# Load order at the start, first units between stages, and the place of the sums in a fused Hyena filter and maxout FFN kernel

## The chip, the cores and the metric

The kernel runs on one core of a Trainium2 chip. The metric is the device time in microseconds (us) of one execution. Every operand is fp32.

## What is computed

The reference, cut to what matters (B = 4, S = 12544, D = 128, filter order 64, d_ff 768):

```python
h_mlp = np.maximum(pos_emb @ w1, 0.0) @ w2
window = np.exp(-0.01 * pos)[:, None]
h_filt = h_mlp * window
u = x * v
L = 2 * S
Uf = np.fft.rfft(u, n=L, axis=1)
Hf = np.fft.rfft(h_filt, n=L, axis=0)
y = np.fft.irfft(Uf * Hf[None, :, :], n=L, axis=1)[:, :S, :]
attn = x * y
...
h = np.maximum(np.maximum(attn @ w1, attn @ w2), attn @ w3)   # moe_w1, moe_w2, moe_w3
return h @ w_out
```

So each batch gets a long convolution along the sequence with a filter that an MLP makes from positions, a gate by x, and then a feed-forward layer that takes the elementwise maximum of three products.

## The kernel before, in words

The Fourier transforms are written as matmuls on TensorE (PE): a first transform over one index of the sequence, a twiddled second one for each of 45 pairs of frequencies, the product with the filter's spectrum, a third one, and an inverse. Instructions are issued by hand in program order (`manual_schedule`), so each engine works through its own queue in the order in which the code emits. A load or store belongs to the queue of the engine that issues it: SyncE (SP), ScalarE (ACT) or GpSimd (POOL). VectorE (DVE) issues none. A tile is one buffer of a pool; a new tile waits until the old user of its buffer is done.

**Start (lines 256 to 343, 859 to 905).** Positions (`pos`, in the storage of `specH`) come in eight pieces, four on SP's and four on ACT's queue (L293); `w1` comes ahead of them on ACT's (L289). On POOL's queue come the window, `eye`, `back`, then the tables `f1h` and `f1q` and two copies of `w2` (L283 to L299). PE meanwhile runs warm-up matmuls on zeros (L156 with `pw`), turns the window (`window_back`) and runs three more warm-ups. Then come eight groups `mlp_in(i)` (L332, pos times w1, into two PSUM tiles `pm`), each followed by `mlp_out(i)` on DVE (L340: relu and window, two instructions). After the last one, sixteen "quads" (`first_halves`, L165) transform the filter, and in between the first units of u = x * v of batch 0 are multiplied on DVE (`u_mul`, L365), turned on PE (`turn2`, eight transposes at L370, one ACT copy at L852) and later transformed by quads as well. A unit is a group of 4 channels-by-position blocks; there are 32 units in a batch.

**Filter stage (lines 996 to 1031).** For each of 45 pairs: `s_second`, `s_filter`, `s_store` make and store the filter's spectrum (`hd`), and `g_second`, `g_third` and their DVE and ACT work convolve batch 0 (stored to `zd`). Near its end the first six units of batch 1 (`EARLY = 6`) are loaded and multiplied and four of them turned.

**Drain (lines 1030 to 1042).** After the last pair the code runs `unit(0)` to `unit(5)` (the first transform of those units: `u_first`, L417, ACT copy L426, DVE add and subtract L428), turns units 4 and 5, and folds two weight matrices into `lin` (`fold`, six transposes and six products). Then the pools of this part are closed and the main loop's are opened.

**Main loop (lines 1068 to 1101).** For three batches, 32 tiles each, six slots f in a tile. A tile is loaded (`t_load`: `zt`, `xT`), two tiles ahead; `t_sums` makes its sum and difference (L678 and L679, or L682 with a sign), `t_last` inverts it on PE and gates it with xT on DVE (L700). In slot f, `up` runs eight `hps` matmuls (L156), a relu on ACT (L710) and a maximum on DVE (L713) over three rotating PSUM banks, and `down` four `ops` matmuls for the slot two back. Beside them `conv_steps` has planned the next batch's convolution: a list of steps by slot (192 in a batch), of which units come first, and pairs from slot `s0`. The planner keeps a `load` per slot and puts `q_re`, `q_im` and `q_unfold` (DVE work of a pair) where it is least. The sums of the next tile are emitted at f = 0, ahead of `up`, on POOL as long as units are worked on (`i * NF <= s0`) and on DVE after that; on the last tile of a batch at f = 3. `t_last` follows at f = 3, 4 or 2.

**Last stage (from L1102).** The last batch's FFN, in another form; the change does not touch it.

Of the kernel before, what the change touches and what calls it, by code (L numbers as in the profile page):

```python
# [91 lines left out]
def kernel(  # L92
# [163 lines left out]
    inp0 = fin.enter_context(tc.tile_pool(name="inp0", bufs=3))  # L256
    sml = fin.enter_context(tc.tile_pool(name="sml", bufs=1))
    mps = ExitStack()
    fps = mps.enter_context(tc.tile_pool(name="fps0", bufs=4, space=PSUM))

# [25 lines left out]
    nc.gpsimd.dma_start(eye[:], eye_d)  # L286
    nc.gpsimd.dma_start(back[:].rearrange("p r t -> p (r t)"), back_d)
    for h in range(2):
        nc.scalar.dma_start(w1_sb[64 * h:64 * h + 64], w1[:, :])  # L289
    cuts = (0, 11, 21, 31, HH)  # L290
    for j, (lo_, hi_) in enumerate(zip(cuts, cuts[1:])):
        for h in range(2):
            (nc.scalar if (h + j) % 2 else nc.sync).dma_start(  # L293
                pos[64 * h:64 * h + 64, lo_ * P:hi_ * P],
                posT[:, (h * HH + lo_) * P:(h * HH + hi_) * P])
    nc.gpsimd.dma_start(f1h[:], f1h_d)
    nc.gpsimd.dma_start(w2_in[0:FO], w2[:, :])
    nc.gpsimd.dma_start(w2_in[FO:P], w2[:, :])
    nc.gpsimd.dma_start(f1q[:], f1_d)  # L299
    for r in range(2):  # L300
        nc.scalar.copy(winT[:, r, 0:64], warm[:, 0:64])

    def warm_up(n):

        ps = fps.tile([P, 1024], FP32, tag="cv", name="pw", bufs=2)
        for _ in range(n):
            halves_mm(ps[:, 0:256], warm[:, 0:P], warm[:], True, True)

    def window_back():
        pw = fps.tile([P, 1024], FP32, tag="cv", name="pw", bufs=2)  # L310
# [270 lines left out]
    def conv_steps(b, done):  # L581


        out = []

        def at(slot, late, fn, *args):
            out.append((slot, late, len(out), fn, args))

        per_pair = 170 / (NK + LATE + 0.6 * (NU - done))
        for u in range(done, NU):
            s = (u - done) * 0.6 * per_pair + 9
            at(max(0, int(s) - 9), 0, u_load, b, u)
            at(int(s) - 6, 0, u_mul, u)
            at(int(s) - 5, 0, u_planes, u)
            at(int(s) - 4, 0, u_dma, u)
            at(int(s), 0, u_join, u)
            at(int(s + 1), 1, u_first, u)
        s0 = int((NU - done - 1) * 0.6 * per_pair + 9) + 6  # L600

        def start(x):
            return s0 + int(x // 2 * 2 * per_pair)

        load = [(1.2 if i % NF == 3 else 0.6) + (1.4 if i % NF == 0 and i > s0 else 0)
                for i in range(NT * NF)]
        for x in range(NK + LATE):
            s = start(x)
            load[s] -= 1.2
            load[s + 1 + x % 2] += 1.4  # L610

        def emptiest(among, cost):
            s = min(among, key=lambda i: load[i])
            load[s] += cost
            return s

        for x in range(NK + LATE):
            s, odd = start(x), x % 2
# [24 lines left out]
        return slots, {start(x) + 1 for x in range(NK + LATE)}, s0  # L643


    N = 4 * NB
# [24 lines left out]
                              x[:, 4 * i:4 * i + 8, c, b, :])  # L671
        xTs[b, i], xTs[b, i + 1] = xT[:, 0], xT[:, 1]

    def t_sums(i, eng=nc.gpsimd):
        z0, z1 = zts[i]
        even = hp.tile([N1, 512], FP32, tag="even", name="even", bufs=2)
        if i[0] == 0 or i[1] < NT // 2:
            eng.tensor_tensor(out=even[:], in0=z0, in1=z1, op=ALU.add)  # L678
            eng.tensor_tensor(out=z1, in0=z0, in1=z1, op=ALU.subtract)  # L679
        else:  # L680
            for out, op in ((even[:], ALU.add), (z1, ALU.subtract)):
                nc.vector.scalar_tensor_tensor(out=out, in0=z1, scalar=sign_t[:, 0:1], in1=z0,  # L682
                                               op0=ALU.mult, op1=op)
        zts[i] = even[:], z1

    def t_last(i):
        zt = zts.pop(i)
# [180 lines left out]
    for i in range(9):  # L868
        if i < 8:
            mlp_in(i)  # L870
        if i:
            mlp_out(i - 1)
    w2_order()
    mps.close()
    fps = fin.enter_context(tc.tile_pool(name="fps", bufs=4, space=PSUM))
    for f in range(0, FO, 4):
        quad([hs[:, f + i] for i in range(4)], (f1h[:, 0], f1h[:, 1]), specH[:, :, :, f:f + 4])
        u, k = divmod(f // 4, 4)
        if u < 2:
            if k in (0, 1):  # L880
                u_mul(2 * u + k)
            if k == 2:
                turn2(2 * u)
# [29 lines left out]
    cps = pro.enter_context(tc.tile_pool(name="cps0", bufs=3, space=PSUM))  # L913
    gps = pro.enter_context(tc.tile_pool(name="gps", bufs=2, space=PSUM))
    sps = pro.enter_context(tc.tile_pool(name="sps", bufs=1, space=PSUM))
    free = itertools.cycle([(gps, "g"), (cps, "cv")])

    def bank():
        pool, tag = next(free)
        return pool.tile([P, 512], FP32, tag=tag, name="ps1")  # L920
# [76 lines left out]
    for s in range(NK + 3):  # L997
# [41 lines left out]
    nc.scalar.copy(lin[:], pl[:, 0:D])  # L1039
    unit(4)  # L1040
    unit(5)
    pro.close()


# [22 lines left out]
    late = []  # L1067
    for n, (b, i) in enumerate(tiles[:LAST]):
        if i == 0:
            beside, folds, pairs_from = conv_steps(b + 1, EARLY if b == 0 else 0)  # L1070
        if n == 0:
            t_load(*tiles[0])
            t_load(*tiles[1])
            t_sums(tiles[0], nc.vector)
            t_last(tiles[0])
        for f in range(NF):

            if i < NT - 2:
                if f == 0:
                    t_load(*tiles[n + 2])  # L1080
            elif i == NT - 1 and f < 2 and n + 1 + f < len(tiles):
                t_load(*tiles[n + 1 + f])
            turn_ = i == NT - 1
            if f == 0:
                when = 4 if turn_ else min((3, 4, 2), key=lambda k: i * NF + k in folds)
# [112 lines left out]
```

## Time and profile before

| what | value |
|---|---|
| median of 4 runs | 2300.31 us (2297.01 to 2306.36) |
| the profiled execution's own time | 2300.47 us |
| its span, first to last instruction | 2298.7 us |
| granted TensorE clock, mean | 0.996 |
| busy: PE, DVE, ACT, POOL | 2265.9, 1573.7, 1175.2, 883.1 us |
| DMA moved | 411.03 MB, mean 179 GB/s |

Stages by the span's own clock, from the stretches that the profile was asked for:

| stretch | what | PE busy | DMA share |
|---|---|---|---|
| 0 to 18.7 | loads, warm-up | 13.32 | 0.91 |
| 18.7 to 35.6 | pos times w1, relu | 14.38 | 0.72 |
| 35.6 to 118 | quads: filter and batch 0 | 80.45 | 0.78, then 0.71 |
| 118 to 150 | filter stage | 32.00 | 0.72 |
| 150 to 262 | filter stage | 111.02 | 0.93 |
| 262 to 291 | filter stage, its end | 28.14 | 0.92 |
| 291 to 314 | drain | 16.92 | 0.49 |
| 314 to 1851 | main loop | 1530.33 | 0.89 to 0.92 |
| 1851 to 2298 | last stage | 439.30 | 0.23 |

How to read it: times are in us from the first instruction. A line of groups or of the timeline names the line of the code, engine, operation and tiles; a bracket gives the idle time just before, and what ended it. A wait is inferred from semaphores, so where several things were waited for the one named may not be the one that mattered. A clock of 1.00 is PE's full clock, 0.50 half of it.

### The profile page before, as it was taken

Reading aid. Unit: us, or ns where it says so; the run is one execution under the profiler, and the core shown is the slowest. Engines: PE = TensorE matmul, PEld = TensorE weight load, DVE = VectorE, ACT = ScalarE, POOL = GpSimd, SP = SyncE. Lnnn points to the kernel's source line nnn. Section 1 sums busy time; section 2 is a strip of 40 time slices with the busy share of each in tenths; the row PEclk is TensorE's granted clock in tenths of the full one; section 3 lists DMA queues with packets and bytes.
Section 4 is the critical chain, followed back from the end, with each engine's and each line's share of the span. In section 5 each row is a group of like instructions: output and inputs, shape, how many; then the busy total and the mean of one; then the engine's idle time right before and its main releaser. Section 6 shows DMA issues by size and latency. Waiting matters only on the chain.

```text
span 2298.7 us, 68542 instructions
## 1 busy us (share of the span) xinstructions
PE 2265.9 (99%) x27855; PEld 1366.7 (59%) x27855; DVE 1573.7 (68%) x2856; ACT 1175.2 (51%) x2128; POOL 883.1 (38%) x1095
## 2 busy tenths in 40 slices
PE   8999989999999999999999999999999999999998
PEld 7988856655555546655555546655555446666665
DVE  5588957667878847758888847758887854445443
ACT  2688834456666534446666624446666622222222
POOL 2044424323333334413333324323333326666666
PEclk9999999999999999999999999999999999999999
DMA  7779979799999669969999759969999832222221
GB/s 186 182 228 278 296 162 185 145 206 246 229 241 229 172 140 191 188 144 243 246 249 249 195 127 198 187 147 238 250 249 245 209 90 55 55 63 67 63 55 22
DMA packets 473166, 411.03 MB, mean 179 GB/s; under 512 B 328006, under 2 KB 374233, under 8 KB 472851
## 3 DMA queue, kind: packets, MB, share of 16 engines
q1 hardware_dynamic: 445954, 329.48, 64.1%
q0 software_dynamic: 26416, 75.80, 11.2%
q8 instruction: 219, 3.59, 0.7%
q10 hardware_dynamic: 480, 1.38, 0.3%
q14 instruction: 97, 0.79, 0.1%
HBM read 262.84 MB, written 84.67 MB: 151 GB/s over the span
## 4 chain that ended last, share of the span: by engine, by line
PE 84%; DMA 11%; DVE 2%; issue 1%; ACT 1%; SPq 1%; POOL 0%; ACTq 0%; DVEq 0%; POOLq 0%
PE hps L156 38%; PE ops L156 16%; PE ops L773 6%; PE cps L417 5%; DMA ht<-hd 3%; PE cps L156 3%; PE ps L165 3%; PE ps L156 3%; PE cps L471 2%; DMA wt<-wq_const 2%; PE cps L481 2%; DMA zt<-zd 2%; DMA hd<-ht 2%; DMA sq<-spec 2%; PE sps L966 1%; PE gps L948 1%
## 5 line engine op out<-in xcount | busy, mean ns | idle before, releaser
L156 PE MATMUL hps<-gt,w_sb 128*64 128x392 f32 x6144 | 1150.6, 495 | 5.7 <-DVE hid L713 4.9
L710 ACT ACTIVATE hid<-hps 128x392 f32<-128x392 f32 x768 | 383.7, 500 | 738.6 <-PE hps L156 721.4
L156 PEld LDWEIGHTS hps<-gt,w_sb 128*64 128x64 f32 x6144 | 423.8, 137 | 438.1 <-issue 392.5
L713 DVE TENSOR_TENSOR hid<-hid,hps 128x392 f32<-128x392 f32 x768 | 427.8, 557 | 335.6 <-PE hps L156 329.9
L156 PE MATMUL ops<-hid,wo_sb 128*64 128x392 f32 x2304 | 478.3, 492 | 0.0
L523 POOL TENSOR_TENSOR cb<-cb,xs 128x512 f32<-128x512 f32 x135 | 181.7, 1346 | 473.2 <-DVE xs L520 331.5
L156 PEld LDWEIGHTS ops<-hid,wo_sb 128*64 128x64 f32 x2304 | 168.4, 137 | 210.8 <-issue 210.8
L496 DVE TENSOR_TENSOR cb<-cps,eo 128x512 f32<-128x512 f32 (+1 forms) x288 | 175.2, 650 | 65.7 <-ACT eo L493 65.2
L428 DVE TENSOR_TENSOR spec<-cps,high 128x360 f32<-128x360 f32 x180 | 135.4, 794 | 122.0 <-ACT high L426 122.0
L728 POOL DMA_DIRECT2D out_dram<-ot x96 | 74.9, 781 | 352.9 <-ACT ot L726 307.7
L511 ACT ACTIVATE xs<-cb 32x512 f32<-32x512 f32 x270 | 169.5, 628 | 22.4 <-DVE cb L496 13.9
L512 ACT COPY xs<-cb 32x512 f32<-32x512 f32 x270 | 166.3, 616 | 3.2
L426 ACT COPY high<-cps 128x360 f32<-128x360 f32 x90 | 71.8, 798 | 152.2 <-PE cps L417 125.5
L527 DVE TENSOR_TENSOR xs<-cb 128x256 f32<-128x256 f32 x270 | 142.0, 569 | 7.5 <-POOL cb L523 7.5
L417 PEld LDWEIGHTS cps<-f1q,uT 98*64 98x64 f32 x2880 | 124.5, 137 | 30.7 <-issue 30.2
L417 PE MATMUL cps<-f1q,uT 98*64 98x90 f32 x2880 | 127.9, 241 | 0.1
L386 POOL COPY planes<-ut 128x784 uint16<-128x784 uint16 x90 | 75.7, 841 | 120.2 <-DVE ut L365 120.2
L504 POOL DMA_DIRECT2D zd<-cb x135 | 92.6, 688 | 61.6 <-DVE cb L496 53.7
L156 PEld LDWEIGHTS cps<-f4p,even 90*64 90x64 f32 x1568 | 89.6, 139 | 37.6 <-issue 36.7
L156 PE MATMUL cps<-f4p,zt 90*64 90x49 f32 x1568 | 97.7, 223 | 1.3 <-DVE zt L679 1.3
L156 PE MATMUL cps<-f4p,even 90*64 90x49 f32 x1568 | 96.3, 221 | 1.9 <-issue 1.9
L515 DVE TENSOR_TENSOR cb<-cb,ht 128x512 f32<-128x512 f32 x135 | 92.2, 683 | 8.4 <-ACT xs L512 7.1
(140 smaller groups left out, 3163.8 us busy)
## 6 DMA issues: line engine op xcount, KB each, us to landing
ht<-hd SPq DMA_DIRECT2D x264, 256.0 KB, 6.8
wt<-wq_const SPq DMA_DIRECT2D x144, 256.0 KB, 6.8
zd<-cb POOLq DMA_DIRECT2D x135, 256.0 KB, 6.4
zt<-zd SPq DMA_DIRECT2D x384, 90.0 KB, 3.0
sq<-spec SPq DMA_DIRECT2D x264, 128.0 KB, 7.0
ut<-in_xr_dram SPq DMA_DIRECT2D x128, 196.0 KB, 4.2
ut<-in_vr_dram SPq DMA_DIRECT2D x128, 196.0 KB, 4.4
xT<-in_x_dram SPq DMA_DIRECT2D x256, 98.0 KB, 3.7
```

The lines of the kernel that those rows point to most:

```text
L156: nc.tensor.matmul(out[64 * h:64 * h + 64], lhsT[:, 64 * h:64 * h + 64], rhs, start=start, stop=stop, skip_group_check=True)
L417: nc.tensor.matmul(ps[64 * c:64 * c + 64, 256 * i + h * N1:256 * i + (h + 1) * N1], t[:, 2 * ((at + i) % 8) + h].rearrange("n r t -> n (r ...
L428: nc.vector.tensor_tensor(out=spec[:, :, a, at:at + n], in0=v[:, 1], in1=high, op=op)
L496: nc.vector.tensor_tensor(out=cb[:, a, lo:hi], in0=ps[:, lo:hi], in1=eo[:, lo:hi], op=op)
L504: nc.gpsimd.dma_start(zd[b][2 * z:2 * z + 2].rearrange("k c t a f -> (k c t) a f"), zss.pop(z))
L511: nc.scalar.mul(xs[at:at + 32], xt[at + 32:at + 64], -1.0)
L512: nc.scalar.copy(xs[at + 32:at + 64], xt[at:at + 32])
L523: nc.gpsimd.tensor_tensor(out=xts[g], in0=xts[g], in1=xs[:], op=ALU.add)
L527: nc.vector.tensor_tensor(out=ab[:, q], in0=y[:, 0], in1=y[:, 1], op=(ALU.subtract, ALU.add)[q])
L710: nc.scalar.activation(h[:], pa[:, 0:N], Relu)
L713: nc.vector.tensor_tensor(out=h[:], in0=h[:], in1=pb[:, 0:N], op=ALU.max)
L773: nc.tensor.matmul(ps[64 * c:64 * c + 64, 0:H2], w, rhs[:, H2 * c:H2 * c + H2], start=start, stop=True, skip_group_check=True)
```

## The change

At the start, `w1` moves from ACT's queue to POOL's, and the tables and `w2` move from POOL's queue to ACT's, where they are issued after the warm-up and the turn of the window. `u_mul` of units 0 and 1 moves between the relu groups, and `turn2(0)` behind the last product group; for this the warm-up's PSUM tiles take the pool's own two buffers.

In the drain, units 0 and 1 go into the filter stage's steps NK and NK + 1. Unit 2's first transform is emitted between the sums and the inverse of the main loop's first tile, unit 3's behind that inverse, and units 4 and 5 in slots 1 and 3 of the loop. The banks are handed out by a fixed list.

In the loop, `conv_steps` returns a plan of three slots for each tile: one for each of the two sums and one for `t_last`. The sums are emitted behind `up`. For tiles with sums on DVE each is put in the emptiest of a few slots, and the `load` counts them there.

```diff
-    fps = mps.enter_context(tc.tile_pool(name="fps0", bufs=4, space=PSUM))
+    fps = mps.enter_context(tc.tile_pool(name="fps0", bufs=2, space=PSUM))
...
-        nc.scalar.dma_start(w1_sb[64 * h:64 * h + 64], w1[:, :])
+        nc.gpsimd.dma_start(w1_sb[64 * h:64 * h + 64], w1[:, :])
...
-    nc.gpsimd.dma_start(f1h[:], f1h_d)
-    nc.gpsimd.dma_start(w2_in[0:FO], w2[:, :])
-    nc.gpsimd.dma_start(w2_in[FO:P], w2[:, :])
-    nc.gpsimd.dma_start(f1q[:], f1_d)
...
+        for u in range(4, done):
+            at(2 * u - 7, 1, u_first, u)
...
-        load = [(1.2 if i % NF == 3 else 0.6) + (1.4 if i % NF == 0 and i > s0 else 0)
-                for i in range(NT * NF)]
+        load = [0.6] * (NT * NF)
...
+        plan = []
+        folds = {start(x) + 1 for x in range(NK + LATE)}
+        for i in range(NT - 1):
+            s = i * NF
+            last = min((3, 4, 2), key=lambda k: s + k in folds)
+            load[s + last] += 0.6
+            if s <= s0:
+                plan.append((0, 0, last))
+                continue
+            a = emptiest(range(s, s + 2), 0.7) - s
+            plan.append((a, emptiest(range(s + a, s + max(a + 1, last - 1)), 0.7) - s, last))
+        plan.append((3, 3, 4))
...
+            two = sorted(emptiest(range(a + 1, last + 1), 0.55) for _ in range(2))
             for q in range(2):
-                at(emptiest(range(a + 1, last + 1), 0.55), 0, q_unfold, g, q)
+                at(two[q], 0, q_unfold, g, q)
...
-    def t_sums(i, eng=nc.gpsimd):
+    def t_sums(i, eng=nc.gpsimd, parts=(0, 1)):
...
     warm_up(3)
+    nc.scalar.dma_start(f1h[:], f1h_d)
+    nc.scalar.dma_start(w2_in[0:FO], w2[:, :])
+    nc.scalar.dma_start(w2_in[FO:P], w2[:, :])
+    nc.scalar.dma_start(f1q[:], f1_d)
     raws.append(load_raw(*jobs[0], nc.sync))
...
             mlp_out(i - 1)
+        if i in (4, 5):
+            u_mul(i - 4)
+        if i == 7:
+            turn2(0)
...
-    free = itertools.cycle([(gps, "g"), (cps, "cv")])
+    def banks_of():
+        for _ in range(2):
+            yield gps.tile([P, 512], FP32, tag="g", name="ps1")[:]
+        both = sps.tile([P, 1024], FP32, tag="h", name="ps1")
+        for h in range(2):
+            yield both[:, 512 * h:512 * h + 512]
+        for pool, tag in ((cps, "cv"), (gps, "g")):
+            yield pool.tile([P, 512], FP32, tag=tag, name="pst")
...
-        if s == NK:
-            unit(0)
+        if s in (NK, NK + 1):
+            unit(s - NK)
...
-    for f, then in enumerate(((unit, 1), (unit, 2), (u_turn, 4), (u_turn, 5), (unit, 3), None)):
+    for f in range(NF):
         folding(f)
-        if then:
-            then[0](then[1])
+        if f in (2, 3):
+            u_turn(f + 2)
...
-    unit(4)
-    unit(5)
...
             t_sums(tiles[0], nc.vector)
+            u_first(2)
             t_last(tiles[0])
+            u_first(3)
...
-            if f == (3 if turn_ else 0):
-                t_sums(tiles[n + 1], nc.vector if turn_ or i * NF > pairs_from else nc.gpsimd)
...
             h = up((b, i), f)
+            for a in range(2):
+                if f == plan[i][a]:
+                    t_sums(tiles[n + 1],
+                           nc.vector if turn_ or i * NF > pairs_from else nc.gpsimd, (a,))
...
-            if f == when:
+            if f == plan[i][2]:
                 t_last(tiles[n + 1])
```

More of the change, by code (lines that the diff above doesn't have):

```diff
@@ L303, in warm_up @@
     def warm_up(n):
-        ps = fps.tile([P, 1024], FP32, tag="cv", name="pw", bufs=2)
+        ps = fps.tile([P, 1024], FP32, tag="cv", name="pw")
         for _ in range(n):
@@ L309, in window_back @@
     def window_back():
-        pw = fps.tile([P, 1024], FP32, tag="cv", name="pw", bufs=2)
+        pw = fps.tile([P, 1024], FP32, tag="cv", name="pw")
         nc.tensor.transpose(pw[:, 0:64 + HH], win[:], eye[0:64 + HH, 0:64 + HH])
@@ L642, in conv_steps @@
             slots.setdefault(s, []).append((fn, args))
-        return slots, {start(x) + 1 for x in range(NK + LATE)}, s0
+        return slots, plan, s0
     N = 4 * NB
@@ L672, in t_load @@
         xTs[b, i], xTs[b, i + 1] = xT[:, 0], xT[:, 1]
-    def t_sums(i, eng=nc.gpsimd):
+    evens_ = {}
+    def t_sums(i, eng=nc.gpsimd, parts=(0, 1)):
         z0, z1 = zts[i]
[L676 to L681, printed above, removed]
+        if 0 in parts:
+            evens_[i] = hp.tile([N1, 512], FP32, tag="even", name="even", bufs=2)
+        even = evens_[i]
+        for a, (out, op) in enumerate(((even[:], ALU.add), (z1, ALU.subtract))):
+            if a not in parts:
+                continue
+            if i[0] == 0 or i[1] < NT // 2:
+                eng.tensor_tensor(out=out, in0=z0, in1=z1, op=op)
+            else:
                 nc.vector.scalar_tensor_tensor(out=out, in0=z1, scalar=sign_t[:, 0:1], in1=z0,
                                                op0=ALU.mult, op1=op)
-        zts[i] = even[:], z1
+        if 1 in parts:
+            zts[i] = evens_.pop(i)[:], z1
     def t_last(i):
@@ L879 @@
         if u < 2:
-            if k in (0, 1):
+            if u and k in (0, 1):
                 u_mul(2 * u + k)
             if k == 2:
-                turn2(2 * u)
+                if u:
+                    turn2(2 * u)
                 for v in range(2 * u + 6, 2 * u + 8):
@@ L915 @@
     sps = pro.enter_context(tc.tile_pool(name="sps", bufs=1, space=PSUM))
-    free = itertools.cycle([(gps, "g"), (cps, "cv")])
+    def banks_of():
[6 more added lines that the diff above has]
+            yield pool.tile([P, 512], FP32, tag=tag, name="pst")
+    free = banks_of()
     def bank():
-        pool, tag = next(free)
-        return pool.tile([P, 512], FP32, tag=tag, name="ps1")
+        return next(free)
     state = {"cv": (cvp, cps), "xb": 2, "bank": bank,
@@ L1069 @@
         if i == 0:
-            beside, folds, pairs_from = conv_steps(b + 1, EARLY if b == 0 else 0)
+            beside, plan, pairs_from = conv_steps(b + 1, EARLY if b == 0 else 0)
         if n == 0:
@@ L1083 @@
             turn_ = i == NT - 1
-            if f == 0:
-                when = 4 if turn_ else min((3, 4, 2), key=lambda k: i * NF + k in folds)
-            if f == (3 if turn_ else 0):
-                t_sums(tiles[n + 1], nc.vector if turn_ or i * NF > pairs_from else nc.gpsimd)
             if f == 4 and n + 1 == LAST:
```

## Prediction

> **What bounds the kernel.** TensorE (PE) is busy in 99% of the span on the page and PE lines carry 84% of the chain that ended last, so I look only for time in which PE waits. I read PE's waits, then the timeline and the clock by stretches at those places. PE's waits (engine and line, releaser: total us, times, longest):
>
> ```profile
> PE hps L156 <- DVE hid L713: 4.9, 10, 0.5
> PE pm L332 <- DMA ut<-in_xr_dram: 3.6, 1, 3.6
> PE ps L156 <- DVE ab L565: 2.1, 1, 2.1
> PE cps L156 <- issue: 1.9, 1, 1.9
> ...
> PE ps L165 <- DVE spec L340: 1.6, 1, 1.6
> PE cps L156 <- DVE zt L679: 1.3, 1, 1.3
> ```
>
> Three places: the start (3.6 and 1.6), the drain between filter stage and main loop (2.1, 1.9, 1.3) and ten half-microsecond stalls in the loop. The change touches all three.
>
> **1. Positions first.** The relu products (L332) start at 18.73; the warm-up ended at 15.16. The releaser named is not the true one: L332 reads pos and w1, and the issue list (size, us from issue to landing) shows the last pos piece, issued on ScalarE's (ACT) queue between 5.2 and 5.8:
>
> ```profile
> specH<-in_pos_emb_dram ACTq DMA_DIRECT2D x1, 320.0 KB, 13.2
> ```
>
> That is 18.5. SyncE's (SP) last piece lands at 2.9 + 11.7 = 14.6: ACT's queue is late because the two w1 loads hold it for 1.24 us (0.74 to 1.98) and the pieces then share the engines with all else. DMA is saturated (share 0.91 over 0 to 18.7). By 15.0 it had moved 3.06 MB (6 us at 142 GB/s, 6 at 240, 3 at 256: 0.85 + 1.44 + 0.77). Pos is 2.69 MB; w1, window, eye and back add 0.20. With the tables (f1h, f1q, w2: 0.36 MB) behind, and both pos queues beginning at 0.74, 2.89 MB are in at about 14.4. The warm-up then sets the start: 15.2 to 15.3.
> Against it stands w1, now fifth on GpSimd's (POOL) queue. There back landed at 3.39 + 9.1 = 12.5, f1h behind it at 14.9, the w2 loads at 16.0 and 16.4. Two 16 KB loads behind back: 1.1 + 0.4 after 12.5 (the steps of the w2 loads), 14.0; 16.4 if they crawl as the loads did in those places. I take a start at 15.6, **gain 3.1**; ends: 0 (w1 at 18.5) and 3.5.
> The Trainium skill ("DMA: Bandwidth & Descriptors", section "Latency and other measured facts") speaks against the move: first byte some 1 us on POOL's path against 0.6 us on ACT's; by that w1 is 0.4 us later than on ACT, and the start gains 3.5. The rows (3.2 us to landing on ACT, 11.4 for w2 on POOL) say the loss is far larger, and they decide.
> The four table loads now issue on ACT at 14.0 to 16.3 (four by 0.53 to 0.57); nothing queues behind them on ACT until the first unit's copy at about 31, and their first reader, L165, comes at about 32. They do delay the first unit loads on SP; u_mul(0) and (1) now stand between the relu outputs on VectorE (DVE). They run at about 24.5 and 26.5; the last of these loads landed at 18.54 + 4.1 = 22.6. The cover is 2 us; without it each late us holds the next L340.
>
> **2. First units turned behind the products.** PE waited 1.58 at 34.03 for the last L340 pair. The eight transposes of units 0 and 1 (1.08, now at 39.48 among the quads) fill this; they cost 1.01 of PE there (39.48 to 40.49). **Gain 1.0.** The two u_muls (0.56 each) go between L340 pairs of 1.3 each, in a cadence of 1.73: 0.13 late each, and gone by the next pair. Low end 0.4: the quads' PSUM pool could wait for the turn's ACT copy (1.01), which ends 0.6 after the last L340.
> Both gains must pass the stages to 291. PE is busy 32.0 of 32.0 and 111.0 of 112.0 there, so a shift passes on; but DMA is at 0.93 from 150 to 262 (a rival below).
>
> **3. Drain.** VectorE's timeline (start, us, instruction; a bracket gives idle before it and what ended it):
>
> ```profile
> 306.68 2.44 DVE L428 TENSOR_TENSOR spec<-ps,high 128x180 f32<-128x180 f32 x8 [1.20 <-ACT high L426]
> 309.04 0.68 DVE L678 TENSOR_TENSOR even<-zt 90x512 f32<-90x512 f32 x1
> 309.75 1.63 DVE L679 TENSOR_TENSOR zt<-zt 90x512 f32<-90x512 f32 x1
> 313.23 0.57 DVE L700 TENSOR_TENSOR gt<-cps,xT 128x392 f32<-128x392 f32 x1 [1.84 <-PE cps L156]
> ```
>
> The first tile's zt landed at 305.1 (second load issued about 301.3, 3.8 to land), but DVE evacuated units 4 and 5 until 309.04. Its second sum took 1.63 instead of 0.68 because POOL summed the second tile from 309.54. And the clock (last three columns: PE clock, DMA share, GB/s):
>
> ```profile
> 308.00:310.00 2.00, 0.18 (x4) 0.21 (x4) 1.96 (x6) 0.47 (x1) 0.46 (x1) 1.00 0.04 8
> 310.00:312.00 2.00, 0.70 (x14) 0.58 (x13) 1.38 (x1) 0.00 (x0) 1.92 (x2) 0.79 0.00 0
> ...
> 314.00:316.00 2.00, 2.00 (x8) 0.84 (x10) 0.00 (x0) 0.32 (x1) 0.00 (x0) 0.50 0.40 100
> 316.00:318.00 2.00, 2.00 (x10) 0.83 (x8) 0.56 (x1) 0.18 (x1) 0.00 (x0) 0.51 0.92 205
> 318.00:320.00 2.00, 2.00 (x16) 0.97 (x14) 0.56 (x1) 0.99 (x2) 0.00 (x0) 1.00 1.21 224
> ```
>
> The idle PE lost half its clock until 318.0, and the 24 hps matmuls from 313.94 took 6.16 where 24 at 0.163 (eight in 1.31 later on) take 3.95.
> After, in before's times: unit 1 fills the 2.1 wait at 293.6; its DVE and ACT work fits before the last zs copy (297.40, held by the zd store), so zt stays at 305.1. Folds and two turns, 0.57 each, run from 298.4 to about 303.3, unit 2 on PE to 304.8. Sums 305.15 to 306.5 at 0.68 each, since POOL's start at 309.5; the inverse transform's last 28 matmuls from 306.56 take 0.82 at full clock (0.117 per four, as at 323.3). On DVE unit 2's two L428 (0.79 each) come next, to 308.1, then gt to 308.7. Unit 3 must wait for unit 2's bank until 308.1, runs 1.33, and the first hps matmul starts at 309.5 instead of 313.94: 4.4. Full clock: 2.2 more. Units 4 and 5 move into the loop, which is PE bound, and cost 2 x 1.33 = 2.7. **Gain 3.9**; ends 0.5 (the clock halves at about 308 and stays so for 6.8 us, as it did from 311.2 to 318.0) and 4.4 (most of unit 3's wait for its bank, 307.4 to 308.1, gone).
> The other edits of the drain (banks by a fixed list, two buffers in the first PSUM pool) I cost at nothing: six bank requests meet six entries, all of banks freed before 303, and without that cover a turn would wait for one copy, 0.6.
> On the clock: here it fell at about 311.2 after 3.3 us in which PE worked 0.3. The Trainium skill ("TensorE: Matmul & The Clock Gate", section "What's actually happening") asks for an idle window of about 3.4 us; by it the drain's new gaps (1.1, 0.3, 0.7) cost nothing and the term stays 3.9, while the row shows that a nearly idle window is enough.
>
> **4. Sums in the loop.** On tiles with DVE sums both (1.36) stand ahead of the first hid max:
>
> ```profile
> 565.82 0.68 DVE L678 TENSOR_TENSOR even<-zt 90x512 f32<-90x512 f32 x1
> ...
> 566.53 0.69 DVE L679 TENSOR_TENSOR zt<-zt 90x512 f32<-90x512 f32 x1
> 567.14 0.55 DVE L713 TENSOR_TENSOR hid<-hid,hps 128x392 f32<-128x392 f32 x1
> ...
> 567.75 1.54 PE L156 MATMUL hps<-gt,w_sb 128*64 128x392 f32 x8 [0.42 <-DVE hid L713]
> ```
>
> Slots of eight hps and four ops matmuls come 1.97 apart; this one took 2.57, so a stall costs 0.60; ten cost 6.0. All are in such tiles, where heavy slots adjoin. After, the max goes first and the sums are placed by load: mostly one in each of two slots. The instruction count is the same. A max must end 2.6 after its product (ops, the next hps, ops: 0.65 + 1.31 + 0.65). Where both sums share a slot, the next max comes behind 1.36 + about 1.4 of planned work + itself 0.56, some 4.2 after the product before, with 4.6 allowed: it holds, unless POOL lengthens a sum by 0.95 as at 309.75. I let ten stalls go and three or four of 0.5 come: **gain 4.0**; ends 0 (as many come as go) and 6.0; fewer than none is rival (e).
>
> **Sum.** 3.1 + 1.0 + 3.9 + 4.0 = 12.0 from the profiled execution's 2300.47 (span 2298.7 and 1.8 around it; 0.16 above the median): **2288.5**. The last stage from 1851 is untouched.
>
> **Rivals.** (a) w1 or a pos piece late: start gains 0.5, 2291.1; for it POOL's rows, against it the 0.36 MB that leave the way. Chance 0.12. (b) The drain's clock halves all the same: 2.2 back, 2290.7; 0.10. (c) The loop's stalls change place, not number: 2292.5; POOL's additions on the same SBUF data speak for it, the loads per slot against it; 0.15. (d) The filter stage is paced by DMA (0.93) and eats the 4.1 of the start: 2292.6; against it PE's 99% there; 0.08. (e) Slower: the sums behind the max stall the next slot in most tiles. 61 tiles have such sums (pairs start at slot 55 of the first batch's 192 and at 62 later, so tiles 10 to 30 once and 11 to 30 twice); 0.60 each is 36.6, against 8.0 of the other terms and 6.0 of old stalls: 2323.1 at worst, and it decides from 24 tiles on. Against it: VectorE is busy 74% of the loop; 0.05. The forecast itself, 2285.5 to 2290.5: 0.50.
>
> **Range and chances.** All upper ends give 15.0, 2285.5; with 1 us of spread between executions, low is 2284.5. High is (a) with (c): 2295. A measurement tells about 0.3% (6.9) from no change: 2293.4 is the bound. All of the forecast, and five sixths of (a) to (d) (0.34 of their 0.45, since two together fall short), are faster: 0.84; same 0.11; slower 0.05.
>
> **What would show it.** Right: L332 starts by 16.0 with no DMA wait over 0.6 before it; eight transposes in the wait before the first quad; the first hps matmul some 8.5 earlier than 313.94 and at clock 1.00; PE's wait on L713 below 2. Wrong: w1's landing past 17; a granted clock of 0.5 in the drain; L713 waits at other tiles; the 4.1 gone again by 291.

## The result

Over all runs of both kernels the change takes 2297.44 us (46 runs, 2292.09 to 2305.39) against 2302.28 (76 runs, 2296.21 to 2313.43); the ratio is 0.9978 with a 95% interval of 0.9973 to 0.9984. That is 4.8 us faster, where 12.0 were forecast, and the median lies above the forecast's range (2284.5 to 2295). The profiled executions stand alike to their medians (2300.47 and 2295.73, 1.8 and 1.7 below), so they can be set side by side: 4.7 us.

### Where the time went

The start of the same matmul in both profiles gives the course of the gain (before minus after, us):

| mark on PE | before | after | gained so far |
|---|---|---|---|
| first relu product | 18.73 | 16.53 | 2.2 |
| first quad of the filter | 35.60 | 35.54 | 0.1 |
| first quad of batch 0 | 58.64 | 56.59 | 2.1 |
| last `s_filter` | 289.34 | 287.37 | 2.0 |
| tile 4 of the loop, second slot | 383.16 | 383.98 | -0.8 |
| tile 95 of the loop | 1860.37 | 1855.61 | 4.8 |

So the start gained 2.0 and kept it, the drain lost 2.8, and the loop gained 5.6. (Of the 2.0 that came between the two first quads, 1.0 are the eight transposes that moved, and 0.7 a gap without a releaser that before's profile has at 57.5.) These are two profiles; e1 to e3 below show how far other profiles of the old order lie from before's. PE's waits in the changed kernel (engine and line, releaser: total us, times, longest):

```profile
PE cps L467 <- DVE gt L717: 6.9, 8, 0.9
PE ps L413 <- DVE spec L424: 3.6, 1, 3.6
PE pm L328 <- issue: 2.9, 3, 1.3
...
PE ps L165 <- ACT uT L869: 1.1, 1, 1.1
```

All the old waits of the list in the prediction are gone (the positions' 3.6, the 2.1 and 1.9 of the drain, the ten on the hidden maximum), and new ones of much the same sum have come. Each of the three places has one.

**The start.** PE's timeline (start, us, instruction; a bracket gives the idle time before it and what ended it):

```profile
16.53 2.99 PE L328 MATMUL pm<-w_sb,specH 64*41 64x64 f32 x114
20.84 3.51 PE L328 MATMUL pm<-w_sb,specH 64*41 64x64 f32 x128 [1.32 <-issue]
24.84 3.46 PE L328 MATMUL pm<-w_sb,specH 64*41 64x64 f32 x128 [0.50 <-issue]
29.39 4.04 PE L328 MATMUL pm<-w_sb,specH 64*41 64x64 f32 x142 [1.09 <-issue]
35.54 8.90 PE L165 MATMUL ps<-f1h,spec 105*64 105x90 f32 x224 [1.10 <-ACT uT L869]
```

The products stand behind no load that the profile names, but the warm-up ends 1.4 later than in before (16.6 against 15.2), because `eye` and `back` land later on POOL's queue (PE waits 0.29 and 1.08 for them). The issue list of the first 36 us (size, us to landing) has w1 on that queue too:

```profile
eye<-eye_const POOLq DMA_DIRECT2D x1, 64.0 KB, 10.3
...
w_sb<-in_w_dram POOLq DMA_DIRECT2D x2, 16.0 KB, 11.8
```

The second of w1's loads was issued at 4.5 and landed at 16.3; the last positions landed at 16.6 (2.9 and 13.6 for the slowest piece). Then come three gaps that nothing released, exactly 128 products apart (2.9 in all, 0.9 in before). The eight turns (33.36 to 34.44) fill the old wait as meant, and the first quad waits 1.10 for their ACT copy.

**The drain.** PE, then VectorE:

```profile
295.81 1.47 PE L413 MATMUL ps<-f1q,uT 98*64 98x90 f32 x16 [3.57 <-DVE spec L424]
...
309.78 2.67 PE L413 MATMUL cps<-f1q,uT 98*64 98x90 f32 x32 [0.55 <-DVE spec L424]
312.20 4.68 PE L156 MATMUL hps<-gt,w_sb 128*64 128x392 f32 x16
```

```profile
306.74 0.69 DVE L696 TENSOR_TENSOR even<-zt 90x512 f32<-90x512 f32 x1 [8.28 <-DMA zt<-zd]
307.46 0.69 DVE L696 TENSOR_TENSOR zt<-zt 90x512 f32<-90x512 f32 x1
```

On VectorE all went as forecast: the sums take 0.69 each, straight behind the landing, unit 2 follows, and gt at 309.55. But the landing is 306.7, not 305.1. The second half of unit 1's first transform stood 3.57 on PE, and behind it the last third transform (297.03), whose store the first tile's load needs. And the clock fell twice, from 295.5 to 298.9 and from 309.1 to 315.9 (the first number behind the length of a stretch is PE's busy time, the last three columns are clock, DMA share, GB/s):

```profile
296.00:298.00 2.00, 2.00 (x26) 2.00 (x26) 0.14 (x1) 0.47 (x1) 0.00 (x0) 0.50 0.03 9
...
310.00:312.00 2.00, 2.00 (x30) 2.00 (x30) 0.11 (x1) 0.00 (x0) 1.61 (x2) 0.50 0.39 99
```

**The loop.** VectorE, then PE, in a tile where both sums share a slot:

```profile
1073.25 2.45 DVE L523 TENSOR_TENSOR xs<-cb 128x256 f32<-128x256 f32 x4
1075.62 0.55 DVE L730 TENSOR_TENSOR hid<-hid,hps 128x392 f32<-128x392 f32 x1
1076.09 0.55 DVE L717 TENSOR_TENSOR gt<-cps,xT 128x392 f32<-128x392 f32 x1
```

```profile
1076.70 0.67 PE L467 MATMUL cps<-sq,wt 64*64 64x128 f32 x16 [0.83 <-DVE gt L717]
```

The inverse `t_last` and two quarters follow each other on PE, and only two pairs of banks go round, so the second quarter needs the bank that gt still has to read. Four unfoldings (L523, 2.45) and a maximum stand ahead of gt. Nine such waits of 0.80 to 0.91 make eight tiles longer by 0.78 to 0.87, and the ninth, where before had one of 0.47 too, by 0.34. The ten old stalls cost about as much: their tiles were longer by 0.64 to 0.77. Eight of the nine stand one tile ahead of an old stall.

### The profile page after: what moved, and what is told of

The parts are those of the page before. It is cut to its first block, busy times and chain, and to the rows that moved or that the text cites. A ratio compares the mean times of both kernels' runs of the same rounds, so it can differ in the third digit from the quotient of the medians.

```text
span 2293.9 us, 68538 instructions
## 1 busy us (share of the span) xinstructions
PE 2260.3 (99%) x27855; PEld 1370.1 (60%) x27855; DVE 1555.6 (68%) x2848; ACT 1174.9 (51%) x2124; POOL 873.4 (38%) x1093
## 4 chain that ended last, share of the span: by engine, by line
PE 87%; DMA 6%; DVE 3%; SPq 1%; issue 1%; ACT 1%; POOL 0%; DVEq 0%; POOLq 0%; ACTq 0%
PE hps L156 40%; PE ops L156 17%; PE ops L790 6%; PE cps L413 5%; PE cps L156 3%; PE ps L156 3%; PE ps L165 3%; PE cps L467 3%; PE cps L477 2%; DMA ht<-hd 2%; PE sps L1000 2%; PE gps L982 1%; DMA hd<-ht 1%; PE last L156 1%; DMA sq<-spec 1%; DVE xs L523 1%
## 5 line engine op out<-in xcount | busy, mean ns | idle before, releaser
L519 POOL TENSOR_TENSOR cb<-cb,xs 128x512 f32<-128x512 f32 x135 | 174.5, 1293 | 470.6 <-DVE xs L516 355.6
L424 DVE TENSOR_TENSOR spec<-cps,high 128x360 f32<-128x360 f32 x188 | 141.3, 793 | 127.4 <-ACT high L422 127.4
L523 DVE TENSOR_TENSOR xs<-cb 128x256 f32<-128x256 f32 x270 | 147.8, 594 | 10.9 <-POOL cb L519 10.9
L413 PEld LDWEIGHTS cps<-f1q,uT 98*64 98x64 f32 x3008 | 131.0, 138 | 32.4 <-issue 31.6
L413 PE MATMUL cps<-f1q,uT 98*64 98x90 f32 x3008 | 135.0, 242 | 1.3 <-DVE spec L424 0.6
L814 POOL DMA_DIRECT2D out_dram<-o x128 | 77.4, 610 | 51.8 <-DVE o L807 49.5
```

Source lines behind the costliest of these rows:

```text
L413: nc.tensor.matmul(ps[64 * c:64 * c + 64, 256 * i + h * N1:256 * i + (h + 1) * N1], t[:, 2 * ((at + i) % 8) + h].rearrange("n r t -> n (r ...
L424: nc.vector.tensor_tensor(out=spec[:, :, a, at:at + n], in0=v[:, 1], in1=high, op=op)
L519: nc.gpsimd.tensor_tensor(out=xts[g], in0=xts[g], in1=xs[:], op=ALU.add)
L523: nc.vector.tensor_tensor(out=ab[:, q], in0=y[:, 0], in1=y[:, 1], op=(ALU.subtract, ALU.add)[q])
```

## The experiments

Medians in us; "before" is the kernel before, run beside it on the same chip.

| kernel | its median | before | ratio, interval |
|---|---|---|---|
| e1 start alone | 2300.01 | 2302.66 | 0.9998, 0.9985 to 1.0010 |
| e2 drain alone | 2304.22 | 2302.66 | 1.0002, 0.9991 to 1.0012 |
| e3 loop alone | 2302.08 | 2302.66 | 0.9994, 0.9981 to 1.0007 |
| e4 change, unit 1 in two banks | 2294.54 | 2302.66 | 0.9964, 0.9949 to 0.9978 |
| e5 e4 with few loads early | 2297.76 | 2304.08 | 0.9972, 0.9961 to 0.9983 |
| e6 e4 with PE kept busy | 2293.07 | 2304.08 | 0.9954, 0.9939 to 0.9969 |
| e7 e4 with an earlier inverse | 2286.90 | 2304.08 | 0.9924, 0.9908 to 0.9941 |
| e8 e4 with the quads' banks open | 2295.13 | 2304.08 | 0.9960, 0.9945 to 0.9975 |
| e9 e4, e7 and e8 together | 2285.64 | 2305.89 | 0.9922, 0.9906 to 0.9938 |
| e10 e9 with PE kept busy | 2282.75 | 2305.89 | 0.9909, 0.9895 to 0.9923 |
| e11 e9 with eye and back first | 2285.33 | 2305.89 | 0.9913, 0.9900 to 0.9926 |
| e12 e9 with the old start, without e8 | 2287.85 | 2305.89 | 0.9929, 0.9917 to 0.9941 |

### e1, e2, e3: one part each

e1 is before with the edits of the start, of which one is

```diff
-        nc.scalar.dma_start(w1_sb[64 * h:64 * h + 64], w1[:, :])
+        nc.gpsimd.dma_start(w1_sb[64 * h:64 * h + 64], w1[:, :])
```

> The kernel before with the edits of the start alone (queues of w1, positions and tables; first units multiplied and turned among the relu products). Theory of parts (each part of the change keeps in this kernel the time it shows in the changed kernel's trace): the products start at about 16.5, end at about 33.4, the first quad starts at about 35.5, and the last product of the filter stage's 45 pairs is 1.9 to 2.1 us earlier than before; total 2.0 us faster (ratio 0.999). Rival (the shift is eaten by the DMA-laden filter stage): the gain at 59 us is 2.1 and at 290 us below 0.7.

e2 is before with the edits of the drain, among them

```diff
-    unit(4)
-    unit(5)
...
+            u_first(2)
             t_last(tiles[0])
+            u_first(3)
```

> The kernel before with the edits of the drain alone (units 0 and 1 in the filter stage's last steps, 2 and 3 around the first inverse, 4 and 5 in the loop). Theory: the second half of unit 1 waits some 3.5 us for VectorE because both halves lie in one PSUM tile; the last third-transform starts some 1.4 us later than before instead of at the same time, the clock halves, and after units 4 and 5 the loop runs 2.6 us behind: total 2.6 us slower. Rival (the loss comes only with the earlier start, by what collides in DMA): total within 1 us of before.

e3 is before with the edits of the loop, among them

```diff
+            for a in range(2):
+                if f == plan[i][a]:
+                    t_sums(tiles[n + 1],
+                           nc.vector if turn_ or i * NF > pairs_from else nc.gpsimd, (a,))
```

> The kernel before with the loop's edits alone (sums behind the products, placed by the plan). Theory: the loop gives 5.4 us in the changed kernel's trace between its second tile and the last stage, and does so here: total 5.4 us faster (ratio 0.9977). Rival (the loop's gain hangs on the moved units or on a changed phase of the loads): less than 2.5 us.

No part alone can be told from no change by its time, and for e3 that is a miss: the 0.9977 expected of it lies outside its interval. The profiles say more.

**Loop.** From tile 4 to 95 the loop of e3 gained 2.7 on before, half of what was expected; with the five other kernels that have the change's loop as it is (after 5.6, e4 4.1, e5 2.8, e6 4.9, e8 3.5) the mean is 3.9. The spread goes with DMA: a few waits on `wq_const` or `sq` where the pairs begin, different in every profile. The old loop spreads too: e1 and e2, which have it, took 1.0 and 1.8 longer than before, with 2.2 and 3.0 of DMA waits where before has 0.7. Against the mean of these three the gain is 4.9.

**Drain.** From the last `s_filter` to tile 4, after lost 2.8 and e2 1.7 on before. But before's drain is the shortest of the three with the old order: in e1 and e3 the same code took 2.6 and 2.4 longer, and there the clock fell behind the old wait of 2.1 as well, at 297.6 and 299.3. The same place in before, and below it in e1 (columns as before):

```profile
294.08:297.50 3.42, 1.84 (x29) 1.48 (x31) 2.69 (x8) 0.62 (x3) 0.24 (x1) 1.00 0.84 211
297.50:300.91 3.41, 3.41 (x69) 2.78 (x65) 1.71 (x6) 2.58 (x8) 0.00 (x0) 1.00 0.42 129
```

```profile
294.21:297.62 3.41, 1.29 (x20) 1.10 (x20) 2.71 (x6) 2.16 (x5) 1.04 (x2) 1.00 0.74 189
297.62:301.04 3.42, 3.42 (x37) 2.77 (x36) 1.06 (x5) 0.75 (x2) 0.00 (x0) 0.50 0.54 157
```

Against the mean of the three old drains, after and e2 lost 0.5 in the mean. So the wait of 3.57 is there in both, as e2's expectation has it, but the larger part of after's 2.8 is the luck of before's profile.

**Start.** It varies most: the last `s_filter` stands at 287.4 (after), 290.8 (e1), 287.6, 287.7 and 288.2 (e4, e6, e7), against 289.3, 290.3, 291.9 and 290.0 with the old start (before, e2, e3, e12): means 288.3 and 290.4, so 2.1 gained, with 3.4 between the best and the worst of the new ones. e1 alone fits neither of its two cases: with 4.5 of gaps in its products its first quad came at 37.4, and its profiled execution is a long one (2305.66 against a median of 2300.01).

### e4: a bank for each half of unit 1

```diff
-        both = sps.tile([P, 1024], FP32, tag="h", name="ps1")
-        for h in range(2):
-            yield both[:, 512 * h:512 * h + 512]
+        yield sps.tile([P, 1024], FP32, tag="h", name="ps1")[:, 0:512]
+        yield cps.tile([P, 512], FP32, tag="cv", name="ps1")[:]
```

> The changed kernel, with the two halves of unit 1 in two separate PSUM tiles (the second one in the rotating tiles of the third transforms). Theory (the second half waits because VectorE still reads the first half of the same tile): the wait of 3.6 us is gone, the last third-transform starts at 293.7 to 294.2 instead of 297.0 or so (in the changed kernel's times), the first tile's zt lands 3 to 3.5 us earlier, and the first hps matmul starts 3 us earlier; total 3 to 5 us faster than the changed kernel. Rival (the second half waits for ScalarE's two copies' buffers, which VectorE frees): the wait stays above 2.5 us.

PE's timeline in e4's drain:

```profile
291.86 1.44 PE L413 MATMUL ps<-f1q,uT 98*64 98x90 f32 x32
...
308.95 4.88 PE L156 MATMUL hps<-gt,w_sb 128*64 128x392 f32 x16
```

Both halves of unit 1 now run in one piece, and the hps matmuls start 3.25 earlier than in after. The tile that they shared made the wait; that is shown. By time e4 and the change lie 3.2 us apart with intervals that touch; the profile carries it. What is left of the drain are waits of 0.4 to 1.2 and the clock: unit 3 still takes 2.67 and sixteen hps matmuls 4.88.

### e6 and e10: PE kept busy

```diff
+            busy(4)
             t_last(tiles[0])
+            busy(2)
             u_first(3)
```

`busy(n)` runs n idle products of a weight matrix with itself, 256 columns wide, into a bank that nobody reads. e10 has them at two more places, ahead of the last third transform and between the first two folds, and fewer at each.

> Kernel: as e4, with idle matmuls of the weights (four pairs ahead of the first tile's inverse, two pairs ahead of unit 3, 0.21 us a pair at full clock, into a bank that nobody reads) in PE's waits of 1.13 and 0.55 us. Nothing is left out. Theory (the clock falls because the 3.4 us before were only half busy): the granted clock stays at 1.00 from 300 to 320, unit 3 takes 1.4 instead of 2.67, the first 16 hps matmuls 2.6 instead of 4.9, and the loop is 3.4 us earlier than in e4 at its first tiles: ratio to before near 0.995. Rival (the fall comes from elsewhere, for example the first wide matmuls after narrow ones): the clock halves near 306 all the same, time as e4 or 0.3 us more.

> Kernel: e9 with idle matmuls at four places of the drain: 0.87 us ahead of the last third transform and between the first two folds (PE waits 0.8 and 1.2 there), 0.87 ahead of the first tile's inverse and 0.43 ahead of unit 3 (waits of 1.1 and 0.55). Nothing is left out. Theory (the clock falls after 3.4 us that are half idle or more, whatever the work is): the granted clock stays at 1.00 from 292 to 320, folds, unit 3 and the first hps matmuls all run at full pace, and the loop's first tiles come 3 us earlier against the last s_filter than in e9 (ratio near 0.9907). Rival (idle matmuls only shift the fall): a stretch of 0.5 of at least 3.3 us between 292 and 320, and a gain below 1.5 us.

In e6 the clock stayed at 1.00 from 302 on, and the sixteen hps matmuls of 4.88 took

```profile
309.70 2.80 PE L156 MATMUL hps<-gt,w_sb 128*64 128x392 f32 x16
```

but it had been at 0.50 from 298 to 301, behind the waits of 0.84, 1.18 and 0.42 at 293 to 298, and the four idle products were twice as long as I had reckoned (1.7, so that the inverse ended some 0.8 late). So the drain gained 1.5 over e4, not 3.4. e10 fills those waits too. Its clock, and below it that of e9, in stretches of 4 us (columns as before):

```profile
300.00:304.00 4.00, 2.93 (x54) 2.20 (x54) 1.70 (x3) 0.79 (x1) 0.00 (x0) 1.00 0.78 187
304.00:308.00 4.00, 3.88 (x72) 2.81 (x70) 2.00 (x4) 1.16 (x2) 2.00 (x2) 1.00 0.51 130
```

```profile
300.00:304.00 4.00, 2.34 (x58) 2.04 (x58) 2.05 (x3) 0.78 (x1) 0.00 (x0) 1.00 0.82 202
304.00:308.00 4.00, 3.44 (x48) 2.98 (x46) 1.27 (x3) 0.35 (x1) 2.39 (x2) 0.58 0.43 123
```

The clock never fell in e10's drain (PE was busy for 66% or more of every 3.41 us of it), and from the last `s_filter` to tile 4 it gained 3.0 on before, where e9 gained 0.7: 2.3 for the clock. So the theory holds, a little smaller than its 3 us. By their times alone e9 and e10 cannot be told apart (their intervals overlap); the profiles carry this one.

### e7: the inverse a slot earlier

```diff
-            last = min((3, 4, 2), key=lambda k: s + k in folds)
+            last = min((3, 4, 2), key=lambda k: s + k in folds or s + k + 1 in folds)
```

> Kernel: as e4, but the planner puts a tile's inverse (t_last) a slot earlier where it would share a slot with two quarters. The change's loop has nine waits of PE for gt, 0.8 to 0.9 us each, in such slots: the second quarter needs the bank that gt reads. Theory A (the bank order makes the wait): the nine waits go, nothing comes for them, and the loop from tile 4 to the last gains 7 us over e4. Theory B (VectorE is behind by some 2 us in these tiles, three to four slots of 2.8 to 3.4 us of work in a row, and the wait only shows where PE next needs it): the waits on gt go but PE waits on the hidden maximum instead in the same tiles, 0.5 to 0.9 each, and the loop gains less than 2 us.

All of PE's waits of the loop that the profile of e7 lists:

```profile
PE cps L467 <- DMA wt<-wq_const: 1.2, 2, 0.7
PE cps L413 <- DVE uT L397: 0.2, 1, 0.2
```

Neither gt nor the hidden maximum is left, so theory A holds and B falls: the bank made the wait. (The planner also places the sums anew around the earlier inverse; that part was not run alone.) The loop gained 12.3 over before, 8.2 more than e4's, and the whole kernel 0.0040 of the ratio (0.9924 against 0.9964). e9, e11 and e12, with the same edit, gained 9.7, 11.4 and 13.4 in their loops; e10 only 6.5, with 4.1 of DMA waits at the quarters in its profile and 3.4 us of half clock at 1041.9.

### e8 and e11: the start's other two limits

```diff
-        ps = fps.tile([P, 1024], FP32, tag="cv", name="ps1")
+        ps = next(turned)
...
-    mps.close()
-    fps = fin.enter_context(tc.tile_pool(name="fps", bufs=4, space=PSUM))
```

> Kernel: as e4, but the PSUM tiles of the start stay open, and the quads use them in turn with the first unit's turn in one of them, so that no quad waits for a whole pool to be given back. Theory (the first quad's wait of 1.1 us on the turn's ACT copy is the pool given back, not data): the wait on the ACT copy goes, PE then waits 0.4 to 0.6 for the last relu on VectorE, and the first quad starts 0.5 to 0.7 us earlier after the last product. Rival (the copy is needed in any case): 1.0 to 1.1 us on the copy as before. Time 0.5 us below e4, which this measurement alone can't tell.

```profile
33.27 1.56 PE L368 MATMUL pw<-eye,ut 128*98 128x128 f32 x8
34.76 1.46 PE L165 MATMUL pm<-f1h,spec 105*64 105x90 f32 x32
```

From the turns to the first quad it is 1.49 instead of 2.18, with the turns at half clock here (30.9 to 34.3), and 1.01 in e9, e10 and e11 at full clock. No wait on the ACT copy is left, nor the 0.4 to 0.6 for the last relu that was expected: 0.7 to 1.2 gained. The pool that was given back made that wait. e11 then moves two loads:

```diff
-    nc.gpsimd.dma_start(eye[:], eye_d)
-    nc.gpsimd.dma_start(back[:].rearrange("p r t -> p (r t)"), back_d)
+    nc.sync.dma_start(eye[:], eye_d)
+    nc.scalar.dma_start(back[:].rearrange("p r t -> p (r t)"), back_d)
```

> Kernel: e9 with eye at the head of SP's queue and back at the head of ACT's, both ahead of the positions, instead of on POOL's. Theory (in the change the warm-up's end sets the start of the products, and it is late because eye and back land at 13.2 and 14.5): the warm-up ends by 12.5, the waits on eye and back go, and PE waits for positions or w1 instead. If positions and w1 could be had at the forecast 15.6 or before, the products start there, 0.9 us earlier. Rival (positions and w1 land at 16 to 16.5 all the same, since the bytes set it): the products start at 16.3 to 17.0 behind a wait of 3 us or more, and nothing is gained; the rival seems likelier.

```profile
17.46 6.42 PE L330 MATMUL pm<-w_sb,specH 64*41 64x64 f32 x242 [1.05 <-issue]
```

`eye` and `back` landed within 2.1 us of their issue, yet the warm-up still ended at 16.4 (14.89 and 1.51 for its last twelve), because its first 88 matmuls alone lasted to 13.5 in this profile (they took 11.1 to 12.6 us from run to run). So the theory's 12.5 did not come. Then PE stood until 17.46; the slowest piece of the positions took 13.9, issued at 3.4, and landed at 17.26. The rival holds in its outcome, though its wait of 3 us shrank to 1.05 behind the late warm-up. In the four profiles with the old start the products also begin 0.2 after the last positions land (18.52 and 18.73 in before). With the new start the last positions came at 15.8 to 17.3 (nine profiles), 1.4 to 2.9 behind the forecast's 14.4.

### e5: few loads in the first 33 us

```diff
+            if gate:
+                nc.vector.memset(t[:, 0, 0:1], 0.0)
```

> Kernel: as e4, but of the loads that SP issues behind the positions only those of units 0 and 1 stay; raw weights and units 2 to 5 wait for a one-element write by VectorE behind the last relu. So DMA carries 2.4 MB less in the first 33 us and 2.4 MB more after. Theory (the products' gaps with no releaser are PE waiting for its own instructions while the loads hold the DMA engines): the gaps of 1.1 to 1.4 in the relu products go, the products end 2.5 us earlier for the same start (16.9 - 2.5 = 14.4 us from first to last), and gaps of the same kind show up in the quads after 33 us. The positions land earlier too, by 15.0, so the products start at the warm-up's end, 16.5 or before. Rival (the gaps belong to PE's own queue, whatever DMA does): two or three gaps, 2 to 3 us in all, at the same counts of products. Time against e4: anywhere from 2 less to 2 more, since the loads only move.

```profile
28.42 3.46 PE L330 MATMUL pm<-w_sb,specH 64*41 64x64 f32 x128 [0.54 <-issue]
32.15 0.58 PE L330 MATMUL pm<-w_sb,specH 64*41 64x64 f32 x14 [0.27 <-issue]
```

The products began at 18.34, behind twelve warm-up matmuls at half clock, and took 14.3 us with these 0.8 of gaps, as the theory said. But e10, with all its loads, had 0.6, and the other kernels with the new start 1.7 to 4.5; with the old start it was 0.8 to 1.4. One profile does not settle it, and no gaps came in the quads, where the loads then stood. The late units also cost 3.6 in waits on VectorE's products. The positions were not in by 15.0 (a piece landed at 15.6), nor did the warm-up end by 16.5. What makes the gaps stays open.

### e9 and e12: all three mended, with the new start and the old

```diff
-    nc.scalar.dma_start(f1h[:], f1h_d)
-    nc.scalar.dma_start(w2_in[0:FO], w2[:, :])
...
+    nc.gpsimd.dma_start(f1h[:], f1h_d)
+    nc.gpsimd.dma_start(w2_in[0:FO], w2[:, :])
```

> Kernel: the change with the three edits of e4 (a bank of its own for each half of unit 1), e7 (the inverse a slot earlier beside two quarters) and e8 (the quads' PSUM tiles kept open). If the three waits are apart from each other, their gains add: e7's 0.9924 less some 0.7 us, so a ratio near 0.992 (2285 against 2303). If they share a limit, for example DMA through the filter stage, it is no faster than e7 alone.

> Kernel: before with the drain's and the loop's edits, mended as in e4 and e7, so e9 with the start as it was. If the start's edits are worth the 2.0 to 2.5 us that the profiles show at the first quad of batch 0, it is 2.5 to 3 us slower than e9 (with e9's 0.6 at the quads), ratio near 0.993. If the start's gain is lost again in the filter stage, it is as fast as e9 within 1 us.

None of the three waits is left in e9's profile, and its 0.9922 is what was expected; but e7 alone had 0.9924, so the times do not tell whether the gains add. The old start, which has no need of e8's edit, costs 0.0007 more, 1.6 us, less than the intervals can tell, and between e12's two cases. Their profiles lie 4.1 apart at the last `s_filter`, but e9's is an early one among 285.7 to 289.3 (e8 to e11).

## Why the prediction was wrong, point by point

- **Start, 3.1 forecast.** The step "I take a start at 15.6" failed. It was 16.5 in after and 16.2 to 18.3 in the other profiles with the new order. Two things were overlooked. `eye` and `back`, which the warm-up needs, landed later on POOL's queue (13.1 and 14.5 instead of 11.1 and 12.5) once the positions had both other queues from the first. And "2.89 MB are in at about 14.4" did not come: in after the engines had moved 2.7 MB by 14.4 and 3.25 by 16.6, when the last positions landed, and part of that were raw weights and first units that SP issued from 5.1 on. w1, the feared one, landed beside the last positions and no later (16.3). The gaps in the products took 2.4 in the mean of the ten profiles with the new start, and 1.1 in the four with the old.
- **Turn, 1.0 forecast.** The stated low end came: the quads' pool waited for the turn's copy (e8). Start and turn together gained 2.1, not 4.1; in the mean the 2.1 reached the last `s_filter`, so rival (d) was wrong.
- **Drain, 3.9 forecast.** This is the largest miss: 2.2 were lost instead against before (after and e2), 0.5 against the mean of the three old drains. The step "unit 1 fills the 2.1 wait at 293.6" failed, and with it "zt stays at 305.1". I counted banks ("six bank requests meet six entries") and did not see that two entries are halves of one tile, which is waited for as one (e4: 3.2 us). Rival (b) came true besides: the clock fell, and the term's low end of 0.5 is what was left once e4's edit was in (0.4 to 1.3 on before in six of the seven such profiles without idle work, 2.5 in e11, where the half clock lasted 3.4 us instead of 6.8). With the clock held it was 3.0 (e10). Against the mean of the old drains each of these is 1.7 more.
- **Clock.** I weighed one rule of the Trainium skill ("TensorE: Matmul & The Clock Gate", section "What's actually happening"), an idle window of 3.4 us, and the row of before, where a nearly idle one was enough. Both were too mild. In e4 the clock fell at 306.28 behind 3.41 us in which PE worked 1.57:

```profile
302.87:306.28 3.41, 1.57 (x38) 1.14 (x34) 2.75 (x4) 0.78 (x1) 0.00 (x0) 1.00 0.73 190
306.28:309.70 3.42, 3.17 (x36) 2.82 (x38) 0.57 (x2) 0.47 (x1) 2.58 (x3) 0.50 0.40 112
```

- **Loop, 4.0 forecast, 3.9 measured on before, 4.9 on the mean of three old loops.** The size came out by luck; the reason was wrong. "I let ten stalls go and three or four of 0.5 come": ten went (their tiles are 7.2 shorter in all in after), and nine of 0.8 to 0.9 came (7.0 longer), on gt instead of the hidden maximum. That is rival (c) in its number, though not by POOL's additions. I had followed the next maximum behind a shared slot and not gt, on which a bank hangs. What after gained comes mostly from 0.2 to 0.3 in each of eleven tiles, most of them the tile behind an old stall (2.9), and from DMA waits that fall differently (2.0 in tiles 43, 44 and 75). Rival (e) did not come.
- **Sum.** On before, 2.1 - 2.2 + 3.9 = 3.8; on the means of all profiles with the old order, 2.1 - 0.5 + 4.9 = 6.5. Measured are 4.8 (3.7 to 6.2 by the interval), so the parts are known to a microsecond or two. The chances of (a) to (d) were put on one of them failing at a time; (b), (c) and part of (a) came together, with a wait that I had not listed. The 1 us allowed for the spread between executions was too little (before's four runs lay 9.4 apart). Two slips change nothing: the upper ends add to 14.9, not 15.0, and 0.34 is three quarters of 0.45, not five sixths.

## What to carry to other kernels

When work is moved into a wait, follow it through its buffers as well as its engine: a tile that two steps share, a pool that is given back or a bank that goes round can stop PE for longer than the wait that was filled. When stalls come from a backlog on another engine, look for every reader on that engine that hands back a bank, not only for the one that stalls today; here one slot of difference in the plan was worth more than the whole change. PE waits of about a microsecond, close together, cost more than themselves if they bring the clock down; idle matmuls put into them gained 2.3 here (e10 against e9, one profile each). And one profile of the kernel before is a weak base: whether a stage lost or gained a microsecond is read against several.

## What was new about the hardware

- In each of the fourteen profiles the granted clock changed only at times that lie whole multiples of 3.413 us apart (in e9, 304.67 and 1110.22 are 236 such steps apart), wherever the work began. Behind a step in which PE was busy for 47% or less the clock was halved every time (37 steps); behind 47 to 58% in 8 of 15; above 58% never. (The ends of matmuls are modelled, so these shares are not exact.) While PE still had work it stayed at 0.50 for one step or two.
- So the same waits cost the clock in one execution and not in another, by where the steps cut them: before's step at the old wait of 2.1 was busy for 54% and kept the clock, e1's and e3's were busy for 38 and 39% and lost it. In e4, PE was busy for only 42% of the 3.41 us from 293.3, but the two steps that share this time had 61 and 79%, and the clock stayed; in e6, with the same waits, one step had 53% and it fell.
- At the start the clock fell in some executions and not in others with the same code ahead: twelve warm-up matmuls took 1.52 in after and 2.75 to 2.83 in e5, e6, e9 and e10. The relu products, 64 columns wide, hardly notice: 242 took 6.4 at clock 1.00 (e11) and 243 took 6.9 in before, most of it at 0.50.
- PE's unreleased gaps in the relu products lie 128 products apart, that is 256 instructions with their weight loads. The Trainium skill ("Runtime: NRT & Kernel Launch", section "Instruction fetch mechanics") has instructions fetched in blocks of 256 and says that crossing into the next block is mostly hidden; the spacing fits, but here 0.2 to 1.9 us showed at a block. Whether the fetch makes the gap was not settled (e5).
- On POOL's queue a 64 KB load took 8.2 us to land in before and 10.3 in after, with the positions on two other queues; at the head of SP's queue it took 1.9 (e11).
